# Mamba-2 scan ahead of a PReLU MLP: compact states in four column tiles, and states times C in eight 64x32 tiles

## The chip, the cores and the metric

The kernel runs on one core of a Trainium2 chip. All inputs and outputs lie in device memory (HBM). Time is device time in microseconds (us) of one execution; lower is better. TensorE multiplies matrices: a stationary operand (the weights, loaded first) and a moving operand, whose columns stream through; results go to PSUM. VectorE, ScalarE and GpSimd do the elementwise work, and DMA queues move data.

## The reference

Two parts follow each other. The first is a state-space scan (Mamba-2) with 4 batches, 8 heads, 768 tokens, head dimension D = 32 and state dimension N = 16. The kernel cuts the tokens into chunks of 128 (six per batch, 24 in all); the reference uses chunks of 32, with the same sums:

```python
cum = np.cumsum(la, axis=-1)                       # la: log of the decays of the chunk
L = np.exp(cum[:, :, :, None] - cum[:, :, None, :]) * causal
M = np.einsum('bhin,bhjn->bhij', Cc, Bc) * L
y_intra = np.einsum('bhij,bhjd->bhid', M, xc)      # inside the chunk
y_inter = np.einsum('bhin,bhnd->bhid', Cc, state) * np.exp(cum)[:, :, :, None]
y = y_intra + y_inter
decay_from_j = np.exp(cum[:, :, -1:] - cum)
Bx = np.einsum('bhjn,bhjd->bhjnd', Bc, xc) * decay_from_j[:, :, :, None, None]
state = decay_full[:, :, None, None] * state + np.sum(Bx, axis=2)   # (N, D) per head
```

The second is an MLP on the 3072 tokens of 256 features (8 heads x 32): `h = x @ w_in` (256 x 2048), `g = max(h, 0) + alpha * min(h, 0)`, `g @ w_out` (2048 x 256). All numbers are float32.

## The kernel before

Chunks are worked on in pairs: 12 pairs, three per batch. For a pair, the kernel updates the states, transposes B and C, forms the decays by scans on VectorE, multiplies B by C head by head, masks with the decays, and then adds two products in PSUM: states times C, and masked products times x. The result is the input of the MLP, which goes over groups of four chunks. Group 0 uses plain products while weights arrive; the later groups use a Strassen scheme of seven products (lines 785 and 760). The pairs of chunks of the next group are worked on between the steps of the current group.

The eight heads lie over the 128 partitions (row h * 16 + n). The state of a chunk is a tile of 128 partitions. Each half of the partitions holds four heads, and its 128 columns are the four heads' 32 features. The product of B and x in a half therefore also gives blocks of one head's B with another head's x; `hmask` zeroes them.

Updating the states (`nk` is 2, or 1 for the last pair of a batch, whose last state nobody reads):

```python
new = work.tile([P, 2, P], F32, name="state")
sm = work.tile([P, 2, P], F32, name="sm")

def added(dps):
    dps = dps[:, : 2 * Q].rearrange("p (k m) -> p k m", m=P)
    for k in range(nk):
        for w in range(KC):                                   # KC = 2 halves
            ws = slice(64 * w, 64 * w + 64)
            nc.tensor.matmul(dps[ws, k], bn[:, k, ws], xt[:, k, w * P : (w + 1) * P],   # line 478
                             start=True, stop=True, tile_position=(0, 64 * w),
                             skip_group_check=True)
    return dps

def states(dps):
    for k in range(nk):
        old = state.get(b)
        if old is None:
            nc.scalar.copy(out=new[:, k], in_=dps[:, k])       # line 487, first chunk of a batch
        else:
            e = (k + 1) * Q - 1
            nc.vector.scalar_tensor_tensor(out=new[:, k], in0=old, scalar=pf[:, e : e + 1],   # line 490
                                           in1=dps[:, k], op0=ALU.mult, op1=ALU.add)
        state[b] = new[:, k]
    nc.gpsimd.tensor_tensor(out=sm[:, :nk], in0=new[:, :nk],                                   # line 493
                            in1=hmask.unsqueeze(1).to_broadcast([P, nk, P]), op=ALU.mult)
    ...
```

The stationary operand of a matmul is its second argument, the moving one the third. `tile_position=(row, column)` names the part of the 128x128 array that a matmul uses; the shapes in the profile say the same ("128*64" is a tile of 128 rows and 64 columns). Where the pair is one of the later ones (`fine`), the matmuls of `added` for the next pair come straight after those below.

The output of a pair; `y[0]` and `y[1]` lie in two banks of PSUM, one for each half of the heads:

```python
begun = False
for k in range(2):
    if st[k] is not None:                                      # not for the first chunk of a batch
        for w in range(KC):
            ws = slice(64 * w, 64 * w + 64)
            nc.tensor.matmul(y[w][:, k], st[k][ws], cd[ws, k], start=not begun, stop=False,     # line 633
                             tile_position=(64 * w, 0), skip_group_check=True)
        begun = True
for k in range(2):
    for w in range(KC):
        for q in range(4):
            h = 4 * w + q
            nc.tensor.matmul(y[w][32 * q : 32 * q + 32, k], xt[:, k, h * D : (h + 1) * D],      # line 640
                             dec[:, k, h], start=False, stop=True,
                             tile_position=(0, 32 * q), skip_group_check=True)
```

Of the kernel before, what the change touches and what calls it, by code (L numbers as in the profile page):

```python
# [9 lines left out]
F32 = mybir.dt.float32  # L10
U32 = mybir.dt.uint32
U16 = mybir.dt.uint16
ALU = mybir.AluOpType
# [9 lines left out]
def kernel(  # L23
# [25 lines left out]
    nc = tc.nc  # L49
# [4 lines left out]
    batch, H, S, D = x.shape  # L54
    N = B.shape[-1]
    P = 128
    Q = 128
# [6 lines left out]
    KC = d_model // P  # L64
# [23 lines left out]
    work = ctx.enter_context(tc.tile_pool(name="work", bufs=2))  # L88
# [5 lines left out]
    op = ctx.enter_context(tc.tile_pool(name="op", bufs=3))  # L94
# [14 lines left out]
    def ss_tile():  # L109
        if early[0] is None:  # L110
            return ps_s.tile([P, 512], F32, name="ss")
        early[0] += 1
        i = early[0] % (3 if ident_p else 4)
        return ps_s.tile([P, 512], F32, name="ss") if i < 2 else bank(i)
# [175 lines left out]
    hmask = bmask[:, :P]  # L290
# [30 lines left out]
    state = {}  # L321
# [57 lines left out]
    def pair_loads(gp):  # L379

        b, c = divmod(2 * gp, CPB)
        nat, abc, xt, ap = loads["p", gp]

        bn = work.tile([P, 2, H * N], F32, name="bn")
        i, bi = divmod(b, 2)
        pj = prt[i].rearrange("p (b h c) -> p b c h", b=2, h=H)[:, bi, c : c + 2]
        nc.gpsimd.tensor_tensor(
            out=bn.rearrange("p k (h n) -> p k h n", h=H),
            in0=nat[:, 0].rearrange("p k (h n) -> p k h n", h=H),
            in1=pj.unsqueeze(3).to_broadcast([P, 2, H, N]), op=ALU.mult)  # L390
        return bn
# [22 lines left out]
    def spare():  # L414

        return ps_h.tile([P, GT], F32, name="hp", tag="hp")

    def pair(gp):

        b, c = divmod(2 * gp, CPB)  # L420
        nat, abc, xt, ap = loads["p", gp]
# [45 lines left out]

        nk = 1 if last else 2
        st = [masked.get(b)]
        new = work.tile([P, 2, P], F32, name="state")  # L470
        sm = work.tile([P, 2, P], F32, name="sm")

        def added(dps):
            dps = dps[:, : 2 * Q].rearrange("p (k m) -> p k m", m=P)
            for k in range(nk):
                for w in range(KC):
                    ws = slice(64 * w, 64 * w + 64)
                    nc.tensor.matmul(dps[ws, k], bn[:, k, ws], xt[:, k, w * P : (w + 1) * P],  # L478
                                     start=True, stop=True, tile_position=(0, 64 * w),
                                     skip_group_check=True)  # L480
            return dps

# [4 lines that stand above are left out]
                    nc.scalar.copy(out=new[:, k], in_=dps[:, k])  # L487
                else:
                    e = (k + 1) * Q - 1
                    nc.vector.scalar_tensor_tensor(out=new[:, k], in0=old, scalar=pf[:, e : e + 1],  # L490
                                                   in1=dps[:, k], op0=ALU.mult, op1=ALU.add)
                state[b] = new[:, k]
            nc.gpsimd.tensor_tensor(out=sm[:, :nk], in0=new[:, :nk],  # L493
                                    in1=hmask.unsqueeze(1).to_broadcast([P, nk, P]), op=ALU.mult)
            st.extend(sm[:, k] for k in range(nk))
            masked[b] = st[-1]

        if fine:
            bn = bns.pop(gp) if gp in bns else pair_loads(gp)
            dps = added(beside.pop(gp) if gp in beside else ss_tile()[:, : 2 * Q])  # L500
            yield
            states(dps)
            yield
# [13 lines left out]
        cd = work.tile([P, 2, Q], F32, name="cd")  # L517
# [16 lines left out]
        if gp == 0:  # L534
            rows_turn(0, held.pop("pr"))
            bns[0] = pair_loads(0)
            dps = spare()
            keep_warm(dps, 6, Q)
            yield
        if not fine:  # L540
            bn = bns.pop(gp) if gp in bns else pair_loads(gp)
        if gp == 1:
            c_decayed()
            dps = spare()
# [4 lines left out]
        if fine:  # L549
            for k in range(2):  # L550
                for w in range(2):
                    half_decays(k, w)
                    if k == 1 and w == 1:
                        spread_c()
                        c_decayed()
                    yield
        else:
            if gp > 1:
                states(added(ss_tile()))
                c_decayed()  # L560
            decays(0)
            if gp == 1:
                dps = added(dps)
            if gp:
                yield
            if gp != 1:
                decays(1)
            if gp > 1:
                spread_c()
# [24 lines left out]
        if gp == 0:  # L594
            gram = products_bc()
            dps = added(dps)
            yield
            c_decayed()
            times(dec[:, :, :2], one_less(gram))
        elif gp == 1:  # L600
            gram = products_bc()
            g0 = one_less(gram)
            yield
            decays(1)
            states(dps)
            times(dec[:, :, :2], g0)
        else:
            if not fine:
                yield
            gram = products_bc()  # L610
# [12 lines left out]
        y = [t[:, : 2 * Q].rearrange("p (k t) -> p k t", k=2) for t in ys]  # L623
# [4 lines left out]
        begun = False  # L628
        for k in range(2):
            if st[k] is not None:  # L630
                for w in range(KC):
                    ws = slice(64 * w, 64 * w + 64)
                    nc.tensor.matmul(y[w][:, k], st[k][ws], cd[ws, k], start=not begun, stop=False,  # L633
                                     tile_position=(64 * w, 0), skip_group_check=True)
                begun = True
        for k in range(2):
            for w in range(KC):
                for q in range(4):
# [3 lines left out]
                                     tile_position=(0, 32 * q), skip_group_check=True)  # L642
        if fine:
            yield
        g, q = divmod(2 * gp, GC)
# [271 lines left out]
    def ssm(gp, stages=1):  # L917

        if gp not in pairs:
            pairs[gp] = pair(gp)  # L920
        for i in range(stages):
            next(pairs[gp], None)
# [115 lines left out]
    for i in range(NZ * (NG - 1)):  # L1038
        g, z = divmod(NZ + i, NZ)
# [71 lines left out]
```

## Time and profile before

The median of three runs is 373.09 us (372.91 to 373.69). The profiled execution spans 371.6 us, with TensorE at its full clock throughout.

| stretch (us) | TensorE busy | VectorE busy | ScalarE busy | GpSimd busy |
|---|---|---|---|---|
| 0 to 20 | 17.80 | 16.61 | 8.10 | 12.91 |
| 20 to 47 | 25.39 | 23.48 | 20.00 | 16.90 |
| 47 to 83 | 35.61 | 30.10 | 17.89 | 24.09 |
| 83 to 150 | 66.81 | 44.43 | 33.08 | 44.17 |
| 150 to 225 | 74.94 | 47.49 | 35.22 | 37.18 |
| 225 to 300 | 74.97 | 51.65 | 35.53 | 38.20 |
| 300 to 340 | 40.00 | 17.58 | 18.68 | 18.60 |

The first 83 us hold the arrival of the weights and group 0, the rest the groups with the Strassen scheme. In the profile's rows a line such as "L478 PE MATMUL ss<-xt,bn" gives the source line, the engine, the operation, and what it writes and reads; "128*64 128x128" is the tile of the array and the moving operand. PE is TensorE's multiplying, PEld its weight loads, DVE is VectorE, ACT ScalarE, POOL GpSimd. The rows of the operations concerned:

| line and engine | what | records | ns |
|---|---|---|---|
| L478 TensorE | state updates | 80 | 272 to 324 |
| L633 TensorE | states times C | 80 | 272 to 373 |
| L640 TensorE | masked products times x | 384 | 272 to 298 |
| L490 VectorE | old state times decay plus update | 16 | 315 to 348 |
| L493 GpSimd | mask of the states | 12 | 455 to 1001 |

Durations of matmuls overlap and include their way through the array; what a stream of them costs is read from the distance of their starts.

### The profile page before, as it was taken

To read this page: it belongs to the slowest core of one execution; us is meant where nothing else is said; L and a number is where in the kernel's file an instruction comes from. 1 tells how busy PE (TensorE), PEld (TensorE's weight loads), DVE (VectorE), ACT (ScalarE), POOL (GpSimd) and SP (SyncE) were. 2 spreads that over 40 slices of the span, in tenths; PEclk is the share of its full clock that TensorE was granted. 3 is DMA by queue.
4 is the path that set the end of the run, shared out by engine and by line. 5 is a ranking of instruction groups with operands and counts; after the bars stand their busy time and mean duration, and the time that the engine had idled before them with its cause. 6 is when DMAs were issued, how large, how long until landed. Compare 5 with 4: busy or idle time off the path is not lost.

```text
span 371.6 us, 6171 instructions
## 1 busy us (share of the span) xinstructions
PE 363.5 (98%) x2223; PEld 291.6 (78%) x2223; DVE 246.2 (66%) x462; ACT 180.1 (48%) x384; POOL 201.5 (54%) x211
## 2 busy tenths in 40 slices
PE   8989999999999999999999999999999999999996
PEld 7766666578788888788788788788788788888884
DVE  7897979968548647838638738638747644643364
ACT  1647866426345345444445445436436425553541
POOL 4875565779738845625636526437445345264512
PEclk9999999999999999999999999999999999999999
DMA  7889999911084401004603702801801001001004
GB/s 148 182 172 321 264 261 203 190 39 58 29 156 100 84 3 56 2 0 64 149 3 57 156 2 44 171 0 30 175 10 29 2 0 25 6 0 30 0 0 85
DMA packets 121877, 30.71 MB, mean 83 GB/s; under 512 B 93736, under 2 KB 117752, under 8 KB 121848
## 3 DMA queue, kind: packets, MB, share of 16 engines
q1 hardware_dynamic: 116736, 29.74, 35.9%
q10 hardware_dynamic: 5112, 0.59, 1.1%
q8 instruction: 17, 0.28, 0.3%
q14 instruction: 12, 0.10, 0.1%
HBM read 26.98 MB, written 3.34 MB: 82 GB/s over the span
## 4 chain that ended last, share of the span: by engine, by line
PE 83%; DVE 9%; DMA 3%; ACT 2%; issue 1%; ACTq 1%; POOLq 0%; SPq 0%; DVEq 0%
PE hp L785 34%; PE bank L760 32%; PE bank L699 3%; PE hp L661 2%; PE ss L640 2%; PE ss L580 2%; DVE dec L441 2%; DMA rows<-in_a_dram 2%; PE ss L633 1%; DVE wr L239 1%; DMA nat<-in_B_dram 1%; DVE dec L435 1%; PE ss L478 1%; PE hp L676 1%; PE ss L511 1%
## 5 line engine op out<-in xcount | busy, mean ns | idle before, releaser
L828 POOL TENSOR_TENSOR gt<-gt 128x512 f32<-128x512 f32 x58 | 73.8, 1272 | 38.3 <-DVE gt L770 31.6
L760 PE MATMUL bank<-gt,w_out 128*128 128x256 f32 x320 | 82.4, 381 | 0.0
L770 DVE SCALAR_TENSOR_TENSOR gt<-hp,s_mul,gt 128x256 f32<-128x256 f32 x120 | 52.4, 478 | 43.5 <-ACT gt L768 40.8
L768 ACT ACTIVATE gt<-hp,s_alpha 128x256 f32<-128x256 f32 x120 | 50.4, 471 | 48.7 <-PE hp L785 36.5
L760 PEld LDWEIGHTS bank<-gt,w_out 128*128 128x128 f32 x320 | 60.1, 190 | 10.4 <-issue 2.3
L760 PE MATMUL bank<-gt,ws 128*128 128x256 f32 x240 | 59.5, 379 | 0.0
L819 POOL TENSOR_TENSOR gt<-gt 128x512 f32<-128x512 f32 x20 | 25.4, 1272 | 56.9 <-DVE gt L770 56.5
L760 PEld LDWEIGHTS bank<-gt,ws 128*128 128x128 f32 x240 | 45.1, 190 | 5.8
L441 DVE TENSOR_TENSOR_SCAN dec<-abc,bank 128x256 f32<-128x256 f32 x80 | 48.0, 659 | 0.0
L785 PE MATMUL hp<-xs,w_in 128*128 128x256 f32 x160 | 42.3, 387 | 0.0
L785 PE MATMUL hp<-xT,w_in 128*128 128x256 f32 x160 | 41.9, 384 | 0.1
L785 PE MATMUL hp<-xs,ws 128*128 128x256 f32 x160 | 40.7, 382 | 0.0
L793 ACT COPY m<-hp 128x512 f32<-128x512 f32 x20 | 11.7, 586 | 52.5 <-PE hp L785 47.4
L804 DVE TENSOR_TENSOR hp<-hp,u 128x512 f32<-128x512 f32 x20 | 13.8, 692 | 34.5 <-ACT u L802 34.5
L785 PEld LDWEIGHTS hp<-xT,w_in 128*128 128x128 f32 x160 | 29.1, 190 | 7.2 <-ACT hp L814 2.9
L785 PEld LDWEIGHTS hp<-xs,ws 128*128 128x128 f32 x160 | 29.8, 190 | 5.5 <-issue 1.1
L785 PEld LDWEIGHTS hp<-xs,w_in 128*128 128x128 f32 x160 | 29.3, 190 | 6.1 <-issue 1.2
L699 PE MATMUL bank<-w_out,gt 128*128 128x256 f32 x128 | 31.0, 384 | 0.0
L699 PEld LDWEIGHTS bank<-w_out,gt 128*128 128x128 f32 x128 | 23.7, 190 | 6.6 <-issue 3.7
L493 POOL TENSOR_TENSOR sm<-state,bmask 128x256 f32<-128x256 f32 (+1 forms) x12 | 8.0, 663 | 34.8 <-DVE state L490 34.6
L661 PE MATMUL hp<-xT,w_in 128*128 128x512 f32 x48 | 22.8, 597 | 0.6 <-DVE gt L665 0.3
L770 DVE SCALAR_TENSOR_TENSOR gt<-c,s_mul,gt 128x256 f32<-128x256 f32 x40 | 20.8, 560 | 0.0
(156 smaller groups left out, 548.8 us busy)
## 6 DMA issues: line engine op xcount, KB each, us to landing
abc<-z SPq DMA_DIRECT2D x20, 512.0 KB, 5.1
raw<-in_moe_w_in_dram SPq DMA_DIRECT2D x8, 512.0 KB, 5.5
raw<-in_moe_w_out_dram SPq DMA_DIRECT2D x8, 512.0 KB, 6.9
xt<-in_x_dram SPq DMA_DIRECT2D x24, 128.0 KB, 3.1
out_dram<-o_sb SPq DMA_DIRECT2D x32, 64.0 KB, 1.9
nat<-in_B_dram SPq DMA_DIRECT2D x22, 64.0 KB, 3.3
nat<-in_C_dram SPq DMA_DIRECT2D x22, 64.0 KB, 2.8
ap<-pf SPq DMA_DIRECT2D x11, 128.0 KB
```

The source lines that it names most:

```text
L441: nc.vector.tensor_tensor_scan(out=dv[:, k, hs], data0=abc[k][:, hs], data1=ident_p[0], initial=0.0, op0=ALU.mult, op1=ALU.add)
L493: nc.gpsimd.tensor_tensor(out=sm[:, :nk], in0=new[:, :nk], in1=hmask.unsqueeze(1).to_broadcast([P, nk, P]), op=ALU.mult)
L661: nc.tensor.matmul(hp, w_in[:, k, f * P : (f + 1) * P], xts[g][:, k], start=(k == 0), stop=(k == KC - 1))
L699: nc.tensor.matmul(pos[0][t // 2][:, t % 2], gt[:, t * Q : (t + 1) * Q], w_out[:, f], start=(f == 0 and t % 2 == 0), stop=(f == NF - 1), s ...
L760: nc.tensor.matmul(ms[g][i][:, h], w, blocks[g, z][n][:, p], start=(q == 0 and h == 0), stop=(q == NQ - 1), skip_group_check=True)
L768: nc.scalar.mul(o[:, p], h[:, p], s_alpha[:, fs[p]])
L770: nc.vector.scalar_tensor_tensor(out=o[:, p], in0=h[:, p], scalar=s_mul[:, fs[p]], in1=o[:, p], op0=ALU.mult, op1=ALU.max)
L785: nc.tensor.matmul(to[:, p], w(2 * z + p), b, start=start and p == 0, stop=True, skip_group_check=True)
L793: nc.scalar.copy(out=m1, in_=A)
L804: nc.vector.tensor_tensor(out=Y, in0=Y, in1=u2, op=ALU.add)
L819: nc.gpsimd.tensor_tensor(out=tc_, in0=g22, in1=g12, op=ALU.subtract)
L828: eng.tensor_tensor(out=o, in0=x0, in1=x1, op=ALU.subtract)
```

## The change

The states become compact: instead of four heads' features side by side in each half, a quarter of the partitions (32 rows, two heads) keeps the 64 features of its own two heads. The state update is done in four column tiles of 32 columns, each with 64 columns of x, instead of two of 64 with 128. The update on VectorE (or the copy on ScalarE) then handles 64 columns. The mask on GpSimd spreads the compact state out to the same block-diagonal tile of 128 columns as before, reading it twice. The products of the states with C are cut into four column tiles for each half, eight tiles of 64 rows and 32 columns, instead of two of 64 rows and 128 columns. The aim is to have more of the array work at a time on these small products, and less for VectorE to do. Nothing else changes.

```diff
--- before.py
+++ after.py
@@ -467,16 +467,17 @@
 
         nk = 1 if last else 2
         st = [masked.get(b)]
-        new = work.tile([P, 2, P], F32, name="state")
+        new = work.tile([P, 2, 2 * D], F32, name="state")
         sm = work.tile([P, 2, P], F32, name="sm")
 
         def added(dps):
-            dps = dps[:, : 2 * Q].rearrange("p (k m) -> p k m", m=P)
+            dps = dps[:, : 4 * D].rearrange("p (k m) -> p k m", k=2)
             for k in range(nk):
-                for w in range(KC):
-                    ws = slice(64 * w, 64 * w + 64)
-                    nc.tensor.matmul(dps[ws, k], bn[:, k, ws], xt[:, k, w * P : (w + 1) * P],
-                                     start=True, stop=True, tile_position=(0, 64 * w),
+                for r in range(4):
+                    rs = slice(32 * r, 32 * r + 32)
+                    nc.tensor.matmul(dps[rs, k], bn[:, k, rs],
+                                     xt[:, k, 2 * r * D : 2 * (r + 1) * D],
+                                     start=True, stop=True, tile_position=(0, 32 * r),
                                      skip_group_check=True)
             return dps
 
@@ -490,8 +491,11 @@
                     nc.vector.scalar_tensor_tensor(out=new[:, k], in0=old, scalar=pf[:, e : e + 1],
                                                    in1=dps[:, k], op0=ALU.mult, op1=ALU.add)
                 state[b] = new[:, k]
-            nc.gpsimd.tensor_tensor(out=sm[:, :nk], in0=new[:, :nk],
-                                    in1=hmask.unsqueeze(1).to_broadcast([P, nk, P]), op=ALU.mult)
+            nc.gpsimd.tensor_tensor(
+                out=sm[:, :nk].rearrange("p k (g m) -> p k g m", g=2),
+                in0=new[:, :nk].unsqueeze(2).to_broadcast([P, nk, 2, 2 * D]),
+                in1=hmask.rearrange("p (g m) -> p g m", g=2).unsqueeze(1)
+                .to_broadcast([P, nk, 2, 2 * D]), op=ALU.mult)
             st.extend(sm[:, k] for k in range(nk))
             masked[b] = st[-1]
 
@@ -628,10 +632,13 @@
         begun = False
         for k in range(2):
             if st[k] is not None:
-                for w in range(KC):
-                    ws = slice(64 * w, 64 * w + 64)
-                    nc.tensor.matmul(y[w][:, k], st[k][ws], cd[ws, k], start=not begun, stop=False,
-                                     tile_position=(64 * w, 0), skip_group_check=True)
+                for q in range(4):
+                    qs = slice(32 * q, 32 * q + 32)
+                    for w in range(KC):
+                        ws = slice(64 * w, 64 * w + 64)
+                        nc.tensor.matmul(y[w][qs, k], st[k][ws, qs], cd[ws, k], start=not begun,
+                                         stop=False, tile_position=(64 * w, 32 * q),
+                                         skip_group_check=True)
                 begun = True
         for k in range(2):
             for w in range(KC):
```

## The prediction

> **What bounds the kernel now.** I read the page first: the busy times and the chain of work that ended last.
>
> ```profile
> PE 363.5 (98%) x2223; PEld 291.6 (78%) x2223; DVE 246.2 (66%) x462; ACT 180.1 (48%) x384; POOL 201.5 (54%) x211
> ...
> PE 83%; DVE 9%; DMA 3%; ACT 2%; issue 1%; ACTq 1%; POOLq 0%; SPq 0%; DVEq 0%
> PE hp L785 34%; PE bank L760 32%; PE bank L699 3%; PE hp L661 2%; PE ss L640 2%; PE ss L580 2%; DVE dec L441 2%; DMA rows<-in_a_dram 2%; PE ss L633 1%; DVE wr L239 1%; DMA nat<-in_B_dram 1%; DVE dec L435 1%; PE ss L478 1%; PE hp L676 1%; PE ss L511 1%
> ```
>
> TensorE carries 83% of the chain and no other engine is over 66% busy. The lines of the change are L478 (state updates) and L633 (states times C), and L490 on VectorE: one or two per cent each. A busy PE hides short gaps, so I went to the timeline of TensorE alone, at a place where the products of states with C (L633), the masked products with x (L640) and a full-array operation follow each other. Columns: start in us, duration, engine, line, operation.
>
> ```profile
> 52.80 0.37 PE L633 MATMUL ss<-cd,sm 64*128 64x128 f32 x1
> 52.80 0.37 PE L633 MATMUL bank<-cd,sm 64*128 64x128 f32 x1
> 53.01 0.27 PE L633 MATMUL ss<-cd,sm 64*128 64x128 f32 x1
> ...
> 53.12 0.27 PE L633 MATMUL ss<-cd,sm 64*128 64x128 f32 x1
> ...
> 53.23 0.27 PE L633 MATMUL ss<-cd,sm 64*128 64x128 f32 x1
> ...
> 53.44 0.43 PE L640 MATMUL ss<-dec,xt 128*32 128x128 f32 x8
> 53.69 0.40 PE L640 MATMUL bank<-dec,xt 128*32 128x128 f32 x8
> 53.91 0.40 PE L640 MATMUL ss<-dec,xt 128*32 128x128 f32 x8
> 54.12 0.40 PE L640 MATMUL bank<-dec,xt 128*32 128x128 f32 x8
> 54.45 0.66 PE L511 MATMUL ss<-ident,nat 128*128 128x128 f32 x4
> ```
>
> Each float32 matmul leaves two records (80 of L633 for its 40 instructions); I call one a pass. Read the starts, not the durations. One pass of 128 columns takes 0.11 us, and every tile of the array does its own at the same time: two tiles in L633, four in L640 (8 records in 0.22 us). Between the last start of L633 (53.23) and the first of L640 (53.44) lie 0.20 us, not 0.11: changing the shape of the tiles costs some 0.09. And the first pass of L633 takes 0.37 instead of 0.27, since its weights load in the open. The minimum, median and maximum of the three lines show that first load for each shape:
>
> ```profile
> L478 PE MATMUL ss<-xt,bn x64: 272/273/324, 36.8 to 275.9; 128*64 128x128 f32 x64
> L633 PE MATMUL ss<-cd,sm x68: 272/272/373, 14.8 to 303.0; 64*128 64x128 f32 x68
> L640 PE MATMUL ss<-dec,xt x320: 272/273/298, 15.3 to 304.0; 128*32 128x128 f32 x160
> ```
>
> 128 columns of weights in the open: +101 ns; 64: +51; 32: +25. Last, the later half of the kernel, where the three blocks come in a row:
>
> ```profile
> 131.13 0.71 PE L633 MATMUL ss<-cd,sm 64*128 64x128 f32 x8
> ...
> 131.78 1.08 PE L640 MATMUL ss<-dec,xt 128*32 128x128 f32 x32
> ...
> 132.79 0.66 PE L478 MATMUL ss<-xt,bn 128*64 128x128 f32 x8
> ...
> 133.38 0.92 PE L785 MATMUL hp<-xs,w_in 128*128 128x256 f32 x3
> ```
>
> Start to start: 0.65, 1.01, 0.59 us. They follow without a wait; what is lost is loads and changes of shape.
>
> **What the Trainium skill says.** "TensorEngine Tiling (Array Packing)", Tiling Modes, says that a change of mode, not merely of tile, drains TensorE; the trace agrees, 0.09 us each. That page gives 128x32 four tiles and 64x32 eight. Its Instruction Overhead puts about 60 cycles on each matmul and warns against tiling a dimension that is small already; the trace before has no 64-column pass, so this is the open figure. "TensorE: Matmul & The Clock Gate", LDWEIGHTS, gives columns / 1.2 ns for a load: 27, 53 and 107 ns for 32, 64 and 128, against 25, 51 and 101 here. Its Part 3, Measured speedup vs the span model, adds about 4 ns per concurrent tile; in this trace tiles of one pass start about 7 ns apart.
>
> **The change, part by part.** A block costs first load + passes + the stagger of its tiles + drain. L633 before: 101 + 4 x 111 + 7 + 93 = 645 ns, as measured; L640: 25 + 8 x 109 + 20 + 93 = 1010.
>
> *State updates.* Before, two tiles of 64 columns with 128 columns of x: 51 + 4 x 109 + 7 + 93 = 587 ns for two chunks, 369 for one. After, four tiles of 32 columns with 64 columns of x. Passes of 128, 256 and 512 columns are 109, 216 and 429 ns apart, so I take 55 for 64. Two chunks: 25 + 4 x 55 + 20 + 93 = 358, one: 248. That saves 0.229 us in each of 8 pairs of chunks and 0.121 in each of the 4 last pairs of a batch. Four starts 7 ns apart are 28, under 55, so issue shouldn't bind, though the instructions double.
>
> *States times C.* The columns of C that stream are still 128, so the passes stay: the halves become quarters, which lie side by side. Only the first load shrinks, by 76 ns, and the stagger grows from 7 to about 50 (eight tiles). 25 + 4 x 109 + 50 + 93 = 604 against 645: 0.041 us, 0.036 for a single chunk. Here the doubling of L633's records gains almost nothing.
>
> *Change of shape.* The order of the built kernel puts L478 straight behind L640 in seven places from 104 us on. Both are now 128x32, so the drain (93 ns) and the open load (25) between them should go: 7 x 0.118 = 0.83 us.
>
> *Other engines.* The state on VectorE (L490) has 64 columns instead of 128: with 347 ns before, and an estimate of 1 ns per column as in other rows (128x512 at 692, 128x256 at 478), some 65 ns less, sixteen times. GpSimd's masking (L493, median 730 ns) writes the same 256 columns and only reads the state twice. All beside other work from 83 us on.
>
> *What counts.* From 81 us TensorE is without a break. There: L478 five doubles and three singles, 5 x 0.229 + 3 x 0.121 = 1.51; L633 six doubles and three singles, 0.35; seven changes of shape, 0.83. Sum 2.69 us. Before 81 us the chain runs through VectorE (L435, L441) and a load of rows; three or four state operations and one L478 lie on it, worth 0.5 at most. I take 0.3. Together 3.0 us: 373.1 - 3.0 = 370.1.
>
> **Rivals.** *Issue binds.* 64 weight loads and matmuls would have to start in 0.44 us in L633, and 32 in 0.22 in L478. The trace shows starts of tiles 7 ns apart, at the edge of enough, but sustains at most 8 loads and matmuls together in 109 ns (L640). If that rate is the limit, L478 stays at 0.22 us per chunk and L633 doubles to 0.43: 20 chunks x 0.22 = 4.3 us more, 0.83 of it given back: 376 to 377. Against it: after L640's first matmuls the next loads follow at 7 ns, with pauses until the pass ends. I give it 8%.
>
> *A wait takes the gain.* If the full-array matmul after L478 waits on ScalarE's copies, a shorter block only lengthens the wait. The waits from 83 to 340 us show L785's weights waiting for ScalarE thus:
>
> ```profile
> PEld hp L785 <- ACT hp L814: 2.9, 8, 0.4
> ...
> PEld hp L785 <- ACT m L793: 0.6, 3, 0.2
> ```
>
> These are local, a few tenths, at other places; behind L478 the next matmul starts at the 0.20 us of a drain, and the copy it needs (L802) ended at 102.54 in the block around 104 us. So at most a part is lost: 371.
>
> *VectorE and GpSimd as the early bound.* GpSimd's mask holds L633 once, at 14.8 us. If reading the state twice makes it slower, a few tenths are lost early; if it gets faster, they are gained. Result 370 to 370.7.
>
> **Range and chances.** Centre 370.1. If the change of shape saves nothing, 370.9; if early time is lost too, 371.3; if a 64-column pass takes 80 ns, another 0.6 goes. Downward there is only the early gain and less stagger: 369.2. I take 369.0 to 372.2. Two per cent is 7.5 us, beyond every path here: faster 0.01, same 0.97, slower 0.02.
>
> **What would show it.** L478 blocks of 0.36 us (two chunks) and passes 55 ns apart; L633 blocks of about 0.60 with passes still 0.11 apart; from the last L640 to the first L478 about 0.11 instead of 0.20; L490 near 280 ns; the stage from 83 to 340 us shorter by 2.7. Passes of L478 at 0.11 or of L633 over 0.15 would prove me wrong, and so would longer starts of L785 behind shorter L478 blocks.

## The result, and the profile after

The changed kernel takes 369.82 us (369.07 to 370.66, four runs) against 373.32 us in the same session: a ratio of 0.9904, 95% interval 0.9882 to 0.9926, so 2.8 to 4.4 us less. The profiled execution spans 368.6 us instead of 371.6.

The page of the changed kernel: busy times, the chain that ended last by engine, and the same by line.

```profile
PE 360.3 (98%) x2543; PEld 290.3 (79%) x2543; DVE 245.8 (67%) x462; ACT 179.4 (49%) x384; POOL 202.0 (55%) x211
...
PE 83%; DVE 8%; DMA 4%; ACT 2%; POOL 1%; issue 1%; POOLq 0%; SPq 0%; DVEq 0%; ACTq 0%
PE hp L792 34%; PE bank L767 33%; PE bank L706 3%; DMA raw<-in_moe_w_in_dram 3%; PE ss L647 3%; PE ss L584 2%; DVE dec L441 2%; DVE dec L435 2%; DMA rows<-in_a_dram 2%; PE hp L668 1%; PE ss L639 1%; DVE wr L239 1%; PE ss L515 1%; PE hp L683 1%; PE hp L270 1%
```

Lines behind the change have moved by seven: the products of states with C are L639 (L633 before), the masked products with x L647 (L640), the Strassen products L792 and L767 (L785 and L760); the state updates stay at L478. TensorE has 320 more records (2543 for 2223) and is busy 3.2 us less. L478 has left the list of the chain.

Minimum, median and maximum duration of the two changed operations, then the timeline of TensorE at the place that the prediction showed around 131 us (start, duration, engine, line, operation):

```profile
L478 PE MATMUL ss<-xt,bn x128: 219/219/244, 36.7 to 273.0; 128*32 128x64 f32 x128
L639 PE MATMUL ss<-cd,sm x272: 269/269/293, 14.9 to 300.0; 64*32 64x128 f32 x136
```

```profile
130.43 0.67 PE L639 MATMUL ss<-cd,sm 64*32 64x128 f32 x32
131.02 1.08 PE L647 MATMUL ss<-dec,xt 128*32 128x128 f32 x32
131.92 0.41 PE L478 MATMUL ss<-xt,bn 128*32 128x64 f32 x16
132.26 0.91 PE L792 MATMUL hp<-xs,w_in 128*128 128x256 f32 x3
```

The first load of a block now costs 25 ns (244 against 219) and 24 ns (293 against 269). The blocks, start to start, are 0.60, 0.90 and 0.34 us, where they were 0.65, 1.01 and 0.59. The masked products were not touched, and yet their block is 0.11 shorter: this is the drain that has gone.

Whole times scatter by 1 to 2.5 us. For the steps I therefore use a stretch inside one execution: from the state update at about 81 us (81.64 before, 81.81 after) to the last masked products (303.17 and 300.17). TensorE is idle for only 0.3 us there before and 0.1 us after, and a second profile of the changed kernel gives the same stretch to 0.02 us. It shrank from 221.53 to 218.36 us, by 3.16.

### The profile page after: what moved, and what is told of

Same layout as the page of the kernel before. It is cut to its first block, busy times and chain, and to the rows that moved or that the text cites. A ratio compares the mean times of both kernels' runs of the same rounds, so it can differ in the third digit from the quotient of the medians.

```text
span 368.6 us, 6811 instructions
## 1 busy us (share of the span) xinstructions
PE 360.3 (98%) x2543; PEld 290.3 (79%) x2543; DVE 245.8 (67%) x462; ACT 179.4 (49%) x384; POOL 202.0 (55%) x211
## 4 chain that ended last, share of the span: by engine, by line
PE 83%; DVE 8%; DMA 4%; ACT 2%; POOL 1%; issue 1%; POOLq 0%; SPq 0%; DVEq 0%; ACTq 0%
PE hp L792 34%; PE bank L767 33%; PE bank L706 3%; DMA raw<-in_moe_w_in_dram 3%; PE ss L647 3%; PE ss L584 2%; DVE dec L441 2%; DVE dec L435 2%; DMA rows<-in_a_dram 2%; PE hp L668 1%; PE ss L639 1%; DVE wr L239 1%; PE ss L515 1%; PE hp L683 1%; PE hp L270 1%
## 5 line engine op out<-in xcount | busy, mean ns | idle before, releaser
L767 PE MATMUL bank<-gt,w_out 128*128 128x256 f32 x320 | 82.4, 381 | 0.0
L767 PEld LDWEIGHTS bank<-gt,w_out 128*128 128x128 f32 x320 | 60.1, 190 | 10.4 <-issue 2.3
L767 PE MATMUL bank<-gt,ws 128*128 128x256 f32 x240 | 59.5, 379 | 0.0
L767 PEld LDWEIGHTS bank<-gt,ws 128*128 128x128 f32 x240 | 45.1, 190 | 5.8
L792 PE MATMUL hp<-xs,w_in 128*128 128x256 f32 x160 | 42.3, 387 | 0.0
L792 PE MATMUL hp<-xT,w_in 128*128 128x256 f32 x160 | 41.9, 384 | 0.1
L792 PE MATMUL hp<-xs,ws 128*128 128x256 f32 x160 | 40.7, 382 | 0.0
L792 PEld LDWEIGHTS hp<-xT,w_in 128*128 128x128 f32 x160 | 29.1, 190 | 7.2 <-ACT hp L821 2.9
L792 PEld LDWEIGHTS hp<-xs,ws 128*128 128x128 f32 x160 | 29.8, 190 | 5.5 <-issue 1.1
L792 PEld LDWEIGHTS hp<-xs,w_in 128*128 128x128 f32 x160 | 29.3, 190 | 5.6 <-ACT u L809 0.6
```

The source lines that it names most:

```text
L767: nc.tensor.matmul(ms[g][i][:, h], w, blocks[g, z][n][:, p], start=(q == 0 and h == 0), stop=(q == NQ - 1), skip_group_check=True)
L792: nc.tensor.matmul(to[:, p], w(2 * z + p), b, start=start and p == 0, stop=True, skip_group_check=True)
```

## The experiments

Times are medians; "stretch" is the one just defined. The kernel before was timed beside each set: 373.45 us in the first, 373.50 in the second, 373.26 in the third.

| kernel | us | ratio to before (95%) | stretch, us |
|---|---|---|---|
| before | 373.3 to 373.5 | | 221.53 |
| compact states alone | 370.10 | 0.9913 (0.9900 to 0.9926) | 218.67 |
| eight tiles alone | 372.66 | 0.9984 (0.9975 to 0.9992) | 221.15 |
| four tiles, wide states | 372.10 | 0.9968 (0.9960 to 0.9976) | 220.43 |
| changed, blocks apart | 371.14 | 0.9940 (0.9925 to 0.9955) | 219.32 |
| changed, again | 369.87 | 0.9909 (0.9884 to 0.9935) | 218.35 |
| changed, updates of 32 columns | 369.91 | 0.9906 (0.9887 to 0.9924) | 218.70 |
| changed, products of 64 columns | 371.35 | 0.9949 (0.9932 to 0.9965) | 219.57 |
| changed, products of 32 columns | 378.46 | 1.0133 (1.0112 to 1.0154) | 224.21 |
| before, B on GpSimd later | 373.36 | 1.0003 (0.9992 to 1.0014) | 221.11 |
| changed, B on GpSimd later | 370.06 | 0.9925 (0.9910 to 0.9939) | 218.34 |

### Compact states alone

My theory was the sum of blocks, a block being an unbroken row of passes of one line: its time is its first load, its passes, the stagger (the few ns from one tile's start to the next) and the drain (the extra time before a block of another shape). The first two runs take one half of the change each. This one differs from the changed kernel by:

```diff
-                for q in range(4):
-                    qs = slice(32 * q, 32 * q + 32)
-                    for w in range(KC):
-                        ws = slice(64 * w, 64 * w + 64)
-                        nc.tensor.matmul(y[w][qs, k], st[k][ws, qs], cd[ws, k], ...)
+                for w in range(KC):
+                    ws = slice(64 * w, 64 * w + 64)
+                    nc.tensor.matmul(y[w][:, k], st[k][ws], cd[ws, k], start=not begun, stop=False,
+                                     tile_position=(64 * w, 0), skip_group_check=True)
```

> The compact states in four column tiles alone; the products of states with C stay in two tiles of 64 rows and 128 columns. Theory of blocks (the time is the sum of first loads, passes, stagger and drains on TensorE): the state updates take 0.34 us for two chunks and 0.225 for one behind the masked products, which shrink from 1.01 to 0.90; the products of states with C stay at 0.645. From 81 us on that is 2.4 us less; with some early gain 370.6 to 370.9 (from 373.3). Rival (the eight tiles carry about half of the gain, since they put the whole array to work): 371.5 or more.

It took 370.10 us, less than the 370.6 to 370.9 expected, and the stretch is 2.86 us shorter. Its blocks, on TensorE's timeline:

```profile
129.23 0.71 PE L637 MATMUL ss<-cd,sm 64*128 64x128 f32 x8
129.87 1.08 PE L644 MATMUL ss<-dec,xt 128*32 128x128 f32 x32
130.77 0.41 PE L478 MATMUL ss<-xt,bn 128*32 128x64 f32 x16
131.11 0.48 PE L789 MATMUL hp<-xs,w_in 128*128 128x256 f32 x1
```

0.64, 0.90 and 0.34 us, as expected. The stretch is 0.4 us better than the blocks say; this comes back below.

### Eight tiles alone

The other half, on the kernel before: L633 in eight tiles (the plus side of the change's diff there), states wide as before.

> The eight 64x32 tiles alone, on the kernel before with its wide states. Theory of blocks: the blocks of products go from 0.645 to 0.60 and nothing else moves, 12 x 0.045 at most: 372.8 to 373.1. Rival (the eight tiles carry half of the gain): 371.5.

372.66 us (0.3 to 0.9 us less), just under the 372.8 to 373.1 expected; the stretch is 0.37 us shorter. Between 81 us and its end there are six blocks that went from 0.645 to 0.597 and two from 0.422 to 0.380: 6 x 0.048 + 2 x 0.042 = 0.37. The rival is out: the eight tiles bring a tenth of the gain, although they hold 240 of the 320 added records.

### Four tiles with wide states

This separates the shape of the tiles from the number of columns. In the kernel before, only this changes:

```diff
-                for w in range(KC):
-                    ws = slice(64 * w, 64 * w + 64)
-                    nc.tensor.matmul(dps[ws, k], bn[:, k, ws], xt[:, k, w * P : (w + 1) * P],
-                                     start=True, stop=True, tile_position=(0, 64 * w),
-                                     skip_group_check=True)
+                for r in range(4):
+                    rs = slice(32 * r, 32 * r + 32)
+                    nc.tensor.matmul(dps[rs, k], bn[:, k, rs],
+                                     xt[:, k, (r // 2) * P : (r // 2 + 1) * P],
+                                     start=True, stop=True, tile_position=(0, 32 * r),
+                                     skip_group_check=True)
```

> The kernel before, with its state updates in four column tiles of 32 that still stream 128 columns of x each; the states stay wide, and VectorE, ScalarE and GpSimd do the same work as before. Theory of blocks: no pass gets shorter, but the shape is that of the masked products, so the seven changes of shape and first loads between them go: masked products 0.90, state updates 0.55 behind them (0.33 for one chunk), 0.574 elsewhere. About 1.1 us less: 372.0 to 372.3. Rival (the gain lies in the narrower states, on TensorE's columns and on VectorE, and a change of shape costs nothing of its own): 373.1 to 373.4, with masked products still at 1.01.

372.10 us, and the stretch is 1.09 us shorter, with no pass removed and the same work on all other engines.

```profile
129.79 0.72 PE L634 MATMUL ss<-cd,sm 64*128 64x128 f32 x8
130.43 1.08 PE L641 MATMUL ss<-dec,xt 128*32 128x128 f32 x32
131.33 0.62 PE L478 MATMUL ss<-xt,bn 128*32 128x128 f32 x16
131.88 0.70 PE L786 MATMUL hp<-xs,w_in 128*128 128x256 f32 x2
```

The masked products' block is 0.90 us again, and the state updates take 0.55 instead of 0.59: 16 records of 128 columns in four tiles stream as long as 8 in two, but their weights load in the shadow. Equal shapes that follow each other save a drain.

### The same blocks, apart

The same thing from the other side: the changed kernel, with the next pair's state updates ahead of the products of states with C.

```diff
             beside[gp + 1] = ys[1][:, 2 * Q :]
+            if gp + 1 < NP:
+                ssm(gp + 1)
...
-                    for p in (1, 0, 1):
+                    for p in (0, 1):
```

> The changed kernel, with the state updates of the next pair moved ahead of the products of states with C in the later half, so that a block of another shape lies between masked products and state updates; the work is the same. Theory of blocks: one drain and one open load more in each of seven places, 0.12 to 0.14 us each: 0.8 to 1.0 us more than the changed kernel, 370.6 to 370.9; masked products 1.01 and state updates 0.36 again. Rival (the order doesn't matter, the gain is all in the columns): 369.7 to 370.0.

371.14 us, 1.3 more than the changed kernel and above the 370.6 to 370.9 expected; the stretch, which scatters less, is 0.95 us longer, as expected.

```profile
129.41 0.43 PE L478 MATMUL ss<-xt,bn 128*32 128x64 f32 x16
129.77 0.67 PE L641 MATMUL ss<-cd,sm 64*32 64x128 f32 x32
130.36 1.08 PE L649 MATMUL ss<-dec,xt 128*32 128x128 f32 x32
131.38 0.70 PE L794 MATMUL hp<-xs,w_in 128*128 128x256 f32 x2
```

The masked products are back at 1.01 us and the update at 0.36: 0.113 + 0.024 = 0.137 us in each of seven places is 0.96. This agrees with the sentence in "TensorEngine Tiling (Array Packing)", Tiling Modes, that a change of mode drains TensorE; here the drain is 0.113 us between two blocks of different shape, and nothing between two of the same.

### The changed kernel again

> The changed kernel once more, for a second profile of it: 369.5 to 370.2, with the same blocks to 0.01 us from 83 us on. If the differences of some tenths before 83 us come from the change, they are the same again; if they come from transfers, the steps around 48 us and 94 us differ from those of the first profile.

369.87 us; the blocks are the same to 0.001 us or so, and the stretch is 218.35. Before it, the two profiles differ: the state update at "81 us" starts at 81.81 in the first and at 82.32 in this one, and in the other kernels anywhere from 80.5 to 81.8 (84.0 with products of 32 columns, whose early blocks are longer). That the change costs or gains some tenths there can't be read from these profiles.

### Shorter updates, twice as many

How much further could this be taken? In the changed kernel each update is cut again:

```diff
-                for r in range(4):
-                    rs = slice(32 * r, 32 * r + 32)
-                    nc.tensor.matmul(dps[rs, k], bn[:, k, rs],
-                                     xt[:, k, 2 * r * D : 2 * (r + 1) * D], ...)
+                for c in range(0, 2 * D, 32):
+                    for r in range(4):
+                        rs = slice(32 * r, 32 * r + 32)
+                        nc.tensor.matmul(dps[rs, k, c : c + 32], bn[:, k, rs],
+                                         xt[:, k, 2 * r * D + c : 2 * r * D + c + 32], ...)
```

> The changed kernel, with each state update cut into two matmuls of 32 columns of x instead of one of 64: twice the instructions, the same columns. Theory of columns (a pass costs its columns and about 2 ns): passes 29 ns apart instead of 55, four tiles starting 7 ns apart just fit; the update of two chunks takes 0.35 us behind the masked products, the time stays at 369.8 to 370.2. Rival (a pass has a floor that 64 columns have reached): passes stay at 55 ns, the update takes 0.56, and the time is 2.2 us more, 372.

369.91 us. The block for two chunks is 0.41 us behind the masked products, against 0.34 with 64 columns; the theory of columns said 0.35, the rival's floor 0.56. Neither is right. The two runs with the products cut help to see why.

### Products of 64 and of 32 columns

The products of states with C of the changed kernel, cut into two (c in steps of 64) or four (steps of 32):

```diff
+                for c in range(0, Q, 32):
                 for q in range(4):
...
-                        nc.tensor.matmul(y[w][qs, k], st[k][ws, qs], cd[ws, k], ...)
+                        nc.tensor.matmul(y[w][qs, k, c : c + 32], st[k][ws, qs], cd[ws, k, c : c + 32], ...)
```

> The changed kernel, with each product of states with C cut into two of 64 columns of C: twice the instructions. Eight tiles starting 7 ns apart need 56 ns, a pass of 64 columns 55: issue just fits, the block stays near 0.60 to 0.62, the time at 369.8 to 370.2. If more than the starts limits issue, the block grows by 0.1 or more and the time by over 1 us.

> The changed kernel, with each product of states with C cut into four of 32 columns: four times the instructions, the same columns. If starts 7 ns apart are the limit, a round of eight tiles takes 56 ns where its columns need 29: the block for two chunks goes from 0.60 to about 1.0, and the time rises by 4.2 us to 374. If only the columns count, the block stays at 0.63 and the time at 370.2.

371.35 and 378.46 us. The expectation for 64 columns failed: its block for two chunks takes 0.79 us, not 0.60 to 0.62. With 32 columns it takes 1.22 and not 1.0. First the kernel with 64 columns, then that with 32:

```profile
130.07 0.86 PE L640 MATMUL ss<-cd,sm 64*32 64x64 f32 x64
130.86 1.08 PE L649 MATMUL ss<-dec,xt 128*32 128x128 f32 x32
```

```profile
133.55 1.29 PE L640 MATMUL ss<-cd,sm 64*32 64x32 f32 x128
134.77 1.08 PE L649 MATMUL ss<-dec,xt 128*32 128x128 f32 x32
```

With 32 columns a block for one chunk (32 instructions) takes 0.686 us, one for two (64 instructions) 1.219: 0.533 / 32 = 16.7 ns per instruction, that is, per two weight loads and two passes. In both kernels the first 16 instructions of a block for two chunks start their passes 5 to 8 ns apart on average, and those behind them come at about 17 ns per instruction. The blocks for one chunk with 64 columns have just 16 instructions, and they take 0.384 us, against 0.380 with 128 columns. Starts 7 ns apart, which I had taken for the limit, hold only for such a stock of instructions that lie ready. The update of 32 columns, of 16 instructions too, shows it at most at its end: where it stands alone (58.21 us) its block takes 0.389 us, with rounds of four tiles 31 to 32 ns apart to the end; behind the masked products it takes 0.407, and only its last passes come up to 17 ns apart. I read the slow pace as a limit on the supply of instructions; the runs show the pace, not what sets it. The changed kernel keeps away from it: L639 needs one every 27 ns (eight in two passes of 109 ns), L478 one every 27 ns (four in two passes of 55).

The time of the kernel with 32 columns rose by 8.6 us; its twelve blocks account for 6.2 (12.50 us together instead of 6.30), a single gap without a visible cause inside a Strassen product at 222 us for 1.2, and the port below for 0.3. The rest, 0.9 us, stays open.

### The multiplication of B on GpSimd, later

All kernels with compact states but the one with products of 32 columns have 0.3 to 0.4 us more gain in the stretch than their blocks. Step by step, and those blocks aside, the two traces part at one place: the block of the products of B with C at 94 us takes 1.95 us before and 1.61 after. Ahead of it VectorE sums w_out. First VectorE and GpSimd before:

```profile
92.66 0.88 DVE L770 SCALAR_TENSOR_TENSOR gt<-hp,s_mul,gt 128x256 f32<-128x256 f32 x2 [0.64 <-ACT gt L768]
93.45 1.07 DVE L728 TENSOR_TENSOR w_out<-w_out 128x512 f32<-128x512 f32 x1
```

```profile
93.33 0.64 POOL L387 TENSOR_TENSOR bn<-nat,prt 128x256 f32<-128x256 f32 x1
```

and after:

```profile
92.59 0.88 DVE L777 SCALAR_TENSOR_TENSOR gt<-hp,s_mul,gt 128x256 f32<-128x256 f32 x2 [0.38 <-ACT gt L775]
93.39 0.73 DVE L735 TENSOR_TENSOR w_out<-w_out 128x512 f32<-128x512 f32 x1
```

```profile
93.52 1.09 POOL L387 TENSOR_TENSOR bn<-nat,prt 128x256 f32<-128x256 f32 x1
```

Whoever starts first takes its usual time, and the other takes 0.34 to 0.45 us more. "SBUF — State Buffer", SBUF: two separate sides, says this of the pair of ports that VectorE and GpSimd share: the one that starts first holds it for the whole instruction. The trace agrees for the most part: before, VectorE ends 0.55 us behind GpSimd's end, of the 0.68 that its sum takes alone (below).

Counted from the state update at 81 us, VectorE's sum starts at 11.80 us before and 11.58 after, GpSimd's multiplication at 11.68 and 11.71. So VectorE came 0.22 us earlier and GpSimd did not. VectorE's multiplications ahead of the sum wait for ScalarE, which waits for TensorE, and TensorE is 0.22 us earlier there behind its shorter update. With wide states in four tiles, where that update stays at 0.575 us, VectorE's sum starts at 11.79 and GpSimd is first. The expectation below says that VectorE starts first in all profiles with compact states; with products of 32 columns GpSimd starts first (95.43 against 95.59 us), and the sum takes 1.03 us there too.

I tested the port by moving GpSimd's multiplication away from there, in both kernels:

```diff
-            ahead = nxt + {(0, 9): 1, (2, 9): 2}.get((z, j), NP)
+            ahead = nxt + {(0, 11 if i == 0 else 9): 1, (2, 9): 2}.get((z, j), NP)
```

> The kernel before; only the multiplication of B on GpSimd that stands beside VectorE's sum of w_out in the first group with the Strassen scheme (around 93 us) is moved behind the three sums of that step, so that GpSimd is idle then. In the profile before, GpSimd starts first there and VectorE's sum takes 1.07 us; in all profiles with compact states VectorE starts first and takes 0.73. Theory of the shared port: without the meeting VectorE's sum takes 0.73 here too, and the products of B with C behind it take 1.61 us instead of 1.95, as with compact states: 0.34 us less, 373.1. Rival (VectorE is only earlier because its state operations are shorter): 1.07 and 1.95 as before, 373.4.

> The same move in the changed kernel. Theory of the shared port: VectorE started first there already, so its sum stays at 0.73 us, the products of B with C at 1.61, and the time at 369.8. Rival: with GpSimd out of the way VectorE gets shorter here as well, 369.5 or less.

VectorE's sum in the kernel before, with GpSimd idle beside it:

```profile
93.52 0.68 DVE L728 TENSOR_TENSOR w_out<-w_out 128x512 f32<-128x512 f32 x1
```

0.68 us instead of 1.07. The products of B with C behind it take 1.56 us instead of 1.95, and the stretch is 221.11, 0.42 less; in the changed kernel nothing moves (0.72 us, 218.34). Between the two kernels with the move the stretch differs by 2.76 us, where the blocks say 2.83. So the traces show the mechanism. The whole time does not: 373.1 us was expected, the kernel before with the move takes 373.36 against 373.26, and the interval (0.3 us less to 0.5 more) just leaves out a gain of 0.34. Why stays open; the two profiles of the changed kernel differ by 0.5 us before 81 us alone.

## Why the prediction was right

The time was predicted as 370.1 us (369.0 to 372.2), and 369.82 came out. In the stretch from 81 us on, where a step can be measured to 0.02 us:

| step of the prediction | predicted, us | measured, us | how measured |
|---|---|---|---|
| state updates, passes of 64 columns | 1.51 | 1.50 | 5 x (0.588 - 0.361) + 3 x (0.369 - 0.249), blocks that stand alone |
| change of shape gone, seven places | 0.83 | 0.96 | 7 x (0.113 + 0.024) |
| states times C | 0.35 (0.32 with the right count) | 0.37 | 6 x 0.048 + 2 x 0.042 |
| sum | 2.69 | 2.83 | |
| not predicted: VectorE ahead of GpSimd at the port | 0 | 0.33 | 3.16 - 2.83; the block at 94 us: 1.95 - 1.61 |

- *The blocks.* For state updates 0.358 and 0.248 us were predicted, 0.361 and 0.249 measured. A pass of 64 columns does cost half of one of 128; four tiles start fast enough. For states times C 0.604 was predicted, 0.597 measured: the passes stayed, only the first load went, as said. The prediction counted three blocks for a single chunk in this stretch; there are two, so its own figures give 0.32 us and not 0.35, and 2.65 in all.
- *The change of shape.* Right in kind, and shown from both sides by the wide states and by the blocks apart. Each is worth 0.137 us, where I had 0.118: the step between masked products and updates shrank by 0.113, not 0.093, because the stagger of the four tiles goes along with the drain.
- *Other engines.* L490 (now L491) was to be near 280 ns, and its median is 280. GpSimd's mask kept its time (median 728 after 730), so reading the state twice costs nothing there. That all this lies "beside other work from 83 us on" was wrong at one place: the shorter update on TensorE brought VectorE's sum to the port ahead of GpSimd's multiplication, which the prediction did not see. Otherwise TensorE's blocks account for all of the gain in the stretch, so the shorter work on VectorE brought nothing of its own there.
- *The early part.* I took 0.3 us for it. That is within the scatter of the profiles before 81 us and neither shown nor refuted. For the later stage the prediction said 2.7 us, and the stretch gave 3.16: 0.14 of the difference lies in the blocks and 0.33 at the port. That an effect which the prediction did not see was small enough for its range is luck.
- *Issue.* This rival did not come true, but my reasoning on it was off: I measured the distance to the limit by starts 7 ns apart. The sustained limit is 16.7 ns per instruction of two loads and two passes, and the changed kernel stays at 27.
- *A wait that takes the gain.* It did not happen: behind the shorter updates the Strassen product starts 0.34 us after the first update, and the shortened blocks show in full in the stretch.

No version that I ran is faster than the changed kernel beyond the uncertainty; the compact states alone, at 370.10 us, are within it.

## What to carry to other kernels

Count a small block on TensorE as first load + passes + stagger + drain, from the starts in its timeline; on a bound TensorE this sum came true to 0.2 us in 2.8. Put blocks of the same tile shape next to each other: that saved 0.137 us each time here, for nothing. Cutting the stationary side alone made no pass shorter here: eight tiles brought 0.37 us, from the first load, and four tiles with wide states 1.09, mostly from the shape that they then shared. Passes got shorter where the moving columns got fewer too, and a block did only until its instructions were wanted faster than one per 16.7 ns.

## What the runs showed of the hardware

- Behind the first 16 instructions of a block, float32 matmuls in eight small tiles came one per 16.7 ns (two weight loads and two passes). The first 16 started their passes 5 to 8 ns apart on average. Products of 64 and 32 columns in eight tiles fell to the slow pace; the first kernel took 1.5 us more, and the blocks of the second 6.2 us more.
- A change of tile shape between two blocks of short passes cost 0.113 us of drain here and 24 ns of open load for 32 columns of weights.
- A sum of 128 x 512 in SBUF on VectorE took 0.68 to 0.76 us alone or first, and 1.07 when a multiplication on GpSimd had started 0.12 us ahead of it; in the other order GpSimd's 0.64 us became 1.09. VectorE's arriving 0.22 us earlier, and so first, saved TensorE another 0.34 us.
